# Decode attention with a cached K and V: K chunks scored in pairs, and the last output columns as one 128-wide block

## The chip, the cores and the metric

The kernel runs on one core of one Trainium2 chip. The metric is the device time in microseconds. Of the kernel before, eight runs are known: 1124.01, 1124.99, 1126.15, 1117.40, 1121.30, 1120.12, 1115.57 and 1117.45 us, with a median of 1120.71 us.

## The reference

Eight sequences (B = 8) decode one token each. The model width is D = 448, with 16 query heads, 8 key/value heads, a head size of 256, and 4096 cached positions. Two kinds of block alternate, A, B, A, B, and both A blocks use the same weights and the same caches, as do both B blocks.

```python
def A(x):                                  # x: (8, 1, 448), already normalized
    q = (x @ wq).reshape(8, 1, 16, 256)    # two query heads per key/value head
    scores = q . k_cache / sqrt(256)       # over 4096 positions
    return (softmax(scores) @ v_cache).reshape(8, 1, 4096) @ wo

def B(x):
    h  = gelu(layernorm(x) @ w1)           # then four shifts along a sequence of length 1
    x1 = x + shifted(h) @ w2               # all four shifted groups are zero: x1 = x
    return x1 + gelu(layernorm(x1) @ w3) @ w4

x = x + A(layernorm(x)); x = x + B(layernorm(x))
x = x + A(layernorm(x)); x = x + B(layernorm(x))
```

With one position per sequence each shift moves the only element out, so w1 and w2 take no part. The K and V caches have 128 MB each (134 million bytes), and both passes of A need them.

## The kernel before, in words

**Tasks and items.** There are two passes, one for each A block. A task (ps, b, gp) is pass ps, batch b and a group gp of two key/value heads; there are four groups. Each task has four K chunks and four V chunks of 128 partitions by 4096 bf16 elements, which is 1 MB. The list `items` (L534 to L543) is the order of all the work: a task's K chunks stand alternately with the V chunks of the task before. The tasks of the two passes are interleaved (L507 to L523), so that batch b's second pass comes soon after its first.

**Places.** A chunk lies in one of 15 places (`slots`, L72, `NC` = 15). Eleven chunks of each batch are `kept` (L63): all eight of group 3, and K chunks 0 to 2 of group 2. They stay in their places from the first pass to the second and are not loaded again. One more V chunk (`inner`, L64) is put into PSUM by `away` and brought back by `back`. `emit_loads` (L559) gives the next load in the list the place that has been free for the longest, and issues one DMA on SP's queue. A DMA in this queue waits for its place, and everything behind it in the queue waits too.

**A K item.** VectorE transposes the chunk in 32 by 32 blocks in two halves (`transpose_k`, L584). TensorE multiplies it with q in 32 matmuls of 8 weight columns and N = 128 (`scores`, L594), in four column groups that write to partitions 0, 32, 64 and 96. After every second chunk ScalarE takes the exponential of 256 columns (`exps`, L603). The transposition of these probabilities on TensorE (`transpose_p`, L630) and their copy to `ptw` on ScalarE (L637) are put between the halves of the next task's first scores, where `TURN` says so (L714).

**A V item.** 16 matmuls with N = 256 (`pv`, L649). The last batch's last tasks use another form (`pv_cols`, L663).

**The chain of a batch.** When two of a batch's groups are done in the first pass, `first_half` starts: the division by the sums, the transposition of the result (L412 to L447), and the product with half of wo (`add_cols`, L339). When all four are done, `chain` adds the other half, the whole B block (`mlp`) and the projection of the next q (`project_q`, L285), with a `norm` ahead of B and of the projection. A norm is a sum over partitions on TensorE (L223), small steps on VectorE, a power on GpSimd (L243) and the normalized vector `xb` (L260). These are generators: `step` (L701) advances them a step at a time between items. Each has a number of steps (11 for `first_half`, 40 for `chain`, 25 for `rest`, in the calls of `add_gen`) and a range of items over which they are spread evenly. `rest` (L495) does the product with wo and the B block for batches 0 to 3 after the second pass, once, while batch 7 is in its first pass.

**The last columns.** `add_cols` makes the 448 outputs in columns of 128 partitions: three blocks of 128 weight columns, and 64 + 64 columns for outputs 384 to 447, where the rows of PSUM are split into two halves. It yields after `every` blocks.

```python
for fc in range(5):
    lo, hi = (128 * fc, 128 * fc + 128) if fc < 3 else (384, 448)
    r = y_ps[:, fc, :] if fc < 3 else y_ps[64 * (fc - 3) : 64 * (fc - 2), 3, :]
```

The fourth column of `xT` therefore holds outputs 384 to 447 twice, and the norm's weights `wv` (L136) count each half with one half.

Of the kernel before, what the change touches and what calls it, by code (L numbers as in the profile page):

```python
# [17 lines left out]
def kernel(  # L18
# [50 lines left out]
    psum = ctx.enter_context(tc.tile_pool(name="psum", bufs=1, space=bass.MemoryType.PSUM))  # L69
    ctx.enter_context(tc.manual_schedule())  # L70

    slots = [consts.tile([128, 16 * Dh], BF16, name=f"slot{n}") for n in range(NC)]  # L72


    spare = [slots[-1], slots[-2]]
# [57 lines left out]

    wv = consts.tile([128, 4], FP32, name="wv")
    nc.vector.memset(wv[:, 0:3], 1.0 / D)
    nc.vector.memset(wv[:, 3:4], 0.5 / D)  # L136
    one = consts.tile([128, 1], FP32, name="one")
    nc.vector.memset(one[:], 1.0)
    ones = one[:].to_broadcast([128, 128])
# [44 lines left out]
    def rows_to_cols(row, nb):  # L184

        idn = identb[:nb, :nb]
        ps = room_ps("y", nb)[:, 0 : 4 * nb].rearrange("p (f b) -> p f b", b=nb)
        for fc in range(3):
            nc.tensor.matmul(
                ps[:, fc, :], row[:nb, 128 * fc : 128 * fc + 128], idn, start=True, stop=True  # L190
            )
        for r in range(2):
            nc.tensor.matmul(
                ps[64 * r : 64 * r + 64, 3, :], row[:nb, 384:448], idn, start=True, stop=True
            )
        return ps

    def norm(x, nb, twice):

        def room(name, shape, at):
            n = shape[0] * shape[1]
            if nb < Bn:
                t = chn.tile([128, n * MID], FP32, tag=name)
                ap = t[:, 0 : n * nb]
            else:
                ap = scratch(at, n * nb)
            return ap.rearrange("p (s f b) -> p s f b", s=shape[0], f=shape[1])

        def bc(ap):
            return ap.unsqueeze(1).to_broadcast([128, 4, nb])

        xx = room("xx", (2, 4), 0)
        nc.vector.tensor_mul(xx[:, 0], x, wv[:].unsqueeze(2).to_broadcast([128, 4, nb]))
        nc.vector.tensor_mul(xx[:, 1], xx[:, 0], x)
        xs = room("xs", (1, 2), 512)[:, 0]
        nc.vector.tensor_reduce(
            xs, xx.rearrange("p s f b -> p s b f"), mybir.AxisListType.X, ALU.add
        )  # L220
        yield
        st = room_ps("st", nb).rearrange("p (s b) -> p s b", b=nb)
        nc.tensor.matmul(st, ones, xs, start=True, stop=True)  # L223
        yield
        mv = room("mv", (1, 2), 528)[:, 0]
        nc.vector.tensor_copy(mv, st)
        var = room("var", (1, 1), 608)[:, 0, 0]
        if nb == 1:
            nc.vector.scalar_tensor_tensor(
                var, mv[:, 0], mv[:, 0], mv[:, 1], ALU.mult, ALU.subtract, reverse1=True  # L230
            )
        else:
            nc.vector.tensor_mul(var, mv[:, 0], mv[:, 0])
            nc.vector.tensor_sub(var, mv[:, 1], var)


        ve = room("ve", (1, 2), 544)[:, 0]
        n = 2 if twice else 1
        nc.vector.tensor_scalar(ve[:, 0], var, 0.0, EPS, ALU.max, ALU.add)
        if twice:  # L240
            nc.vector.tensor_scalar(ve[:, 1], var, 0.0, EPS * EPS / (1 + EPS), ALU.max, ALU.add)
        rs = room("rs", (1, 2), 560)[:, 0]
        nc.gpsimd.tensor_tensor(  # L243
            rs[:, 0:n].rearrange("p n b -> p (n b)"),
            ve[:, 0:n].rearrange("p n b -> p (n b)"),
            nhalf[:].to_broadcast([128, n * nb]),
            ALU.pow,
        )
        xc = room("xc", (1, 4), 576)[:, 0]
        nc.vector.tensor_tensor(xc, x, bc(mv[:, 0]), ALU.subtract)  # L250
        yield
        if nb > 1:
            yield
        c = (1 + EPS) ** -0.5 if twice else 1.0
        rl = rs[:, n - 1]
        parts = ((slice(0, 128), 0, 3, 0), (slice(0, 64), 3, 4, 3), (slice(64, 128), 3, 4, 4))
        for pp, f0, f1, to in parts:
            dst = xbs(nb)[pp, to : to + f1 - f0, :]
            if nb == 1:
                nc.vector.tensor_scalar(dst, xc[pp, f0:f1], rl[pp], c, ALU.mult, ALU.mult)  # L260
            else:
                nc.vector.scalar_tensor_tensor(
                    dst,
                    xc[pp, f0:f1],
                    c,
                    rl[pp].unsqueeze(1).to_broadcast([pp.stop - pp.start, f1 - f0, nb]),
                    ALU.mult,
                    ALU.mult,
                )
        if twice and nb == 1:  # L270
            nc.vector.scalar_tensor_tensor(x, xc, rs[:, 0], x, ALU.mult, ALU.add)
        elif twice:
            nc.vector.tensor_tensor(xc, xc, bc(rs[:, 0]), ALU.mult)
            nc.vector.tensor_add(x, x, xc)
        yield
# [51 lines left out]

    def add_cols(y_ps, rhs, w, rows, every, open=None):

        for fc in range(5):  # L330
            lo, hi = (128 * fc, 128 * fc + 128) if fc < 3 else (384, 448)
            r = y_ps[:, fc, :] if fc < 3 else y_ps[64 * (fc - 3) : 64 * (fc - 2), 3, :]
            for i in rows:
                if open is None:
                    start, stop = i == rows[0], i == rows[-1]
                else:
                    start = open[0] and fc == 0 and i == rows[0]
                    stop = open[1] and i == rows[-1]
                nc.tensor.matmul(  # L339
                    r,  # L340
                    w[:, i, lo:hi],
                    rhs(i),
                    start=start,
                    stop=stop,
                    skip_group_check=open is not None,
                )
            if fc % every == every - 1 or fc == 4:
                yield

    def mlp_hidden(b0, nb):  # L350
# [205 lines left out]
    places = list(range(NC))  # L556
    where = {}

    def emit_loads(most=None):  # L559
        n = 0  # L560
        while loads and places and n != most:
            it = loads.pop(0)
            p = where[it] = places.pop(0)
            if stays(it):
                where[tasks[it[0]][1:], it[1:]] = p
            t, kv, c = it
# [16 lines left out]
            w = t[:].bitcast(U32).rearrange("p (y e w) -> p y e w", e=2, w=64)[:, :, half]  # L583
            nc.vector.transpose(w, w)  # L584

    def scores(t, x, qbd, gp, between=None):
        kv = t[:].rearrange("p (k t e i r) -> p k e r t i", k=4, t=4, e=4, r=2)
        for n in range(8):
            half, e2, par = n // 4, (n // 2) % 2, n % 2
            if n == 4 and between is not None:  # L590
                between()
            ep = 4 * e2 + 2 * par + half
            for k in range(4):
                nc.tensor.matmul(  # L594
                    sc[32 * k : 32 * k + 8, 128 * x : 128 * x + 128],
                    qbd[:, ep, gp].rearrange("p a h -> p (a h)"),
                    kv[:, k, 2 * half + e2, par],
                    start=(n == 0),
                    stop=(n == 7),
                )  # L600
# [111 lines left out]
                    gens.remove(e)  # L712

    def TURN(n):  # L714
        return 0

    first_of = {}
    for idx, (n, kv, c) in enumerate(items):
# [3 lines left out]
    for idx, it in enumerate(items):  # L722
        n, kv, c = it
        ps, b, gp = tasks[n]
        if (ps, b, gp, kv, c) == (0, Bn - 1, REST, 0, 0):
            assert pairs_done[1, MID - 1] == 4
            add_gen("rest", 0, rest(), idx + 1, idx + 18, 25)
        p = where[(b, gp), (kv, c)] if ps == 1 and (stays(it) or inside(it)) else where[it]
        slot = slots[p]
        final = (ps, b) == (1, Bn - 1)  # L730
        if kv == 0:
# [20 lines left out]
            turn = None  # L752
            if c == TURN(n) and n - 1 in p_of:
                turn = lambda t=p_of.pop(n - 1): transpose_p(t)
            scores(slot, c, st["q"], gp, between=turn)
            if c == 1:
                p_n = work.tile([128, 4, 32, 4], BF16, tag="p_sb", bufs=1)
                p_of[n] = p_n
# [5 lines left out]
        else:  # L764
# [6 lines left out]
            if final and gp in free:  # L771
                pv_cols(oc, slot, c, gp)
                if c % 2 == 1:
# [7 lines left out]
                            lambda i: OT2[:, i % 2, i // 2, MID:],  # L781
                            wo_sb,
                            range(h0, h0 + 4),
                            5,
                            open=(claim(st), gp == free[-1] and u == 1),
                        )
                    )
# [11 lines left out]
            if c == 3:  # L799
                done = pairs_done[ps, b] = pairs_done.get((ps, b), 0) + 1  # L800
                if done == 2 and ps == 0:
                    add_gen("chain", b, first_half(b, st), idx + 1, idx + 21, 11)
                elif done == 2:
                    add_gen("chain" if final else "last", b, first_last(b, st), idx + 1, idx + 13, 9)
                elif done == 4 and ps == 0:
                    add_gen("chain", b, chain(b, st), idx + 1, first_of[(1, b), 0] - 1, 40)
                elif done == 4 and not final:
                    add_gen("last", b, last(b, st), idx + 1, idx + (7 if b == Bn - 2 else 13), 6)
        if not (ps == 0 and stays(it)):
# [18 lines left out]
    run(mlp_hidden(MID, Bn - MID))  # L828
    for q in range(4):
        for fc in range(4):  # L830
            w = 128 if fc < 3 else 64
            lo, hi = max(W * q, 128 * fc), min(W * q + W, 128 * fc + w)
            if lo < hi:
                nc.tensor.matmul(
                    o_row[32 * q : 32 * q + Bn, lo - W * q : hi - W * q],
                    xT[:w, fc, :],
                    ident2[:w, lo - 128 * fc : hi - 128 * fc],
                    start=(lo == W * q),
                    stop=False,
                    skip_group_check=True,  # L840
# [47 lines left out]
```

## Time and profile before

| | |
|---|---|
| median of eight runs | 1120.71 us |
| the profiled execution | 1124.01 us, its span 1122.2 us |
| busy: PE matmuls, PE weight loads, DVE, ACT | 716.0, 519.0, 591.7, 124.3 us |
| instructions | 36,998, of which PE 2 x 17,173 |
| read from HBM | 446.77 MB, 398 GB/s over the span |
| transposes of K chunks (L584), 400 | 469.2 us, 1219 ns each |
| matmuls of scores (L594), 8192 | 284.4 us busy |
| matmuls of V (L649), 3968 | 249.6 us busy |
| loads of K (200) and V (216), 1 MB each | 11.3 and 10.2 us from issue to landing |

How to read the profile: its page is one execution. "Busy" of an engine is the time in which at least one of its instructions runs, and PE's matmuls and weight loads (PEld) overlap. In the rows by slice each digit is a fortieth of the span in tenths. In a list in order of time a row has its start, its length, the engine, the line of the code, the operation with the names it writes and reads, the count, and in brackets the idle time before it with what ended it. "issue" there means that the engine waited for nothing that the profile shows.

### The profile page before, as it was taken

The numbers are of one execution on the slowest core, as the hardware profiler recorded it, in microseconds if no ns is written. First come the engines' busy times: TensorE is split into PE (matmuls) and PEld (weight loads), VectorE is DVE, ScalarE is ACT, GpSimd is POOL, SyncE is SP. The second block draws the span as 40 slices with busy tenths as digits, with TensorE's granted clock in tenths as the row PEclk, the third lists the DMA queues.
The fourth block names the chain that finished last, engine by engine and source line by source line (L and its number), as shares of the span: only waits on it lengthen the run. The fifth ranks groups of instructions, "written<-read, shape, count | busy, mean of one in ns | idle before, by whom it ended". The sixth has DMA issues, their size and how long they took to land. (4 is left out here: it accounts for less than half of the span.)

```text
span 1122.2 us, 36998 instructions
## 1 busy us (share of the span) xinstructions
PE 716.0 (64%) x17173; PEld 519.0 (46%) x17173; DVE 591.7 (53%) x1009; ACT 124.3 (11%) x362; POOL 15.6 (1%) x25
## 2 busy tenths in 40 slices
PE   3145577756864676636784477745778477877775
PEld 2123355434642454425563255533556355655565
DVE  5155454646465546555365553655537553485462
ACT  0001001110110011101011010110011001011010
POOL 0000000000000000000000000000000000000000
PEclk9999999655575556655556555655555555565575
DMA  9999999999999999999999999999999999999994
GB/s 357 385 419 421 410 381 404 420 411 395 419 420 420 397 410 417 420 420 385 398 419 419 420 379 403 419 420 406 402 400 419 410 396 415 418 359 398 413 418 166
DMA packets 65193, 449.15 MB, mean 400 GB/s; under 512 B 6920, under 2 KB 10896, under 8 KB 11408
## 3 DMA queue, kind: packets, MB, share of 16 engines
q1 hardware_dynamic: 65008, 446.80, 97.9%
q8 instruction: 134, 2.20, 0.8%
q14 instruction: 19, 0.16, 0.0%
q10 hardware_dynamic: 32, 0.00, 0.0%
HBM read 446.77 MB, written 0.01 MB: 398 GB/s over the span
## 5 line engine op out<-in xcount | busy, mean ns | idle before, releaser
L584 DVE STREAM_TRANSPOSE slot<-slot 128x1024 uint32<-128x1024 uint32 x400 | 469.2, 1219 | 256.1 <-DMA slot<-in_A_k_cache_dram 251.2
L594 PE MATMUL sc<-slot,qbd 128*8 128x128 bf16 x8192 | 284.4, 291 | 313.1 <-DVE slot L584 247.5
L594 PEld LDWEIGHTS <-qbd 128*8 128x8 bf16 x8192 | 191.3, 107 | 383.9 <-issue 208.3
L649 PE MATMUL o<-slot,ptw 128*8 128x256 bf16 x3968 | 249.6, 396 | 45.3 <-DMA slot<-in_A_v_cache_dram 36.2
L603 ACT ACTIVATE p_n<-sc 128x256 bf16<-128x256 f32 x128 | 95.4, 746 | 811.1 <-PE sc L594 811.1
L649 PEld LDWEIGHTS <-ptw 128*8 128x8 bf16 x3968 | 112.8, 111 | 87.1 <-issue 52.8
L339 PEld LDWEIGHTS <-wo_sb 128*128 128x128 bf16 (+1 forms) x1600 | 65.3, 123 | 25.9 <-issue 25.1
L339 PE MATMUL misc<-OT,wo_sb 128*128 128x1 bf16 (+1 forms) x1280 | 58.0, 176 | 2.7 <-issue 2.7
L285 PEld LDWEIGHTS <-wq_sb 128*128 128x128 bf16 x1152 | 34.7, 104 | 24.1 <-issue 18.6
L285 PE MATMUL misc<-xb,wq_sb 128*128 128x1 bf16 x1024 | 33.3, 166 | 3.4 <-ACT ptw L637 2.8
L311 DVE TENSOR_SCALAR qbd<-misc,quad 128x64 bf16<-128x64 f32 x64 | 13.8, 277 | 40.3 <-PE misc L305 40.3
L637 ACT CAST ptw<-misc 128x128 bf16<-128x128 f32 x64 | 17.5, 274 | 148.0 <-PE misc L630 81.7
L603 ACT ACTIVATION_READ_ACCUMULATOR p_n<-sc 128x1 f32 x128 | 33.7, 263 | 0.0
L443 PEld LDWEIGHTS misc<-R,o_sb 128*128 128x128 f32 x124 | 28.4, 316 | 10.1 <-issue 8.0
L443 PE MATMUL misc<-R,o_sb 128*128 128x8 f32 x124 | 31.3, 363 | 0.0
L339 PEld LDWEIGHTS <-w_sb 128*128 128x128 bf16 (+1 forms) x630 | 25.0, 125 | 11.0 <-issue 11.0
L243 POOL TENSOR_TENSOR t<-t,nhalf 128x2 f32<-128x2 f32 (+2 forms) x18 | 13.3, 739 | 1093.0 <-DVE t L250 1093.0
L357 PEld LDWEIGHTS <-w_sb 128*128 128x128 bf16 x560 | 18.3, 105 | 18.1 <-issue 18.1
L415 DVE RECIPROCAL rz<-misc 128x8 f32<-128x8 f32 (+1 forms) x33 | 6.3, 190 | 38.0 <-PE misc L412 36.5
L357 PE MATMUL misc<-xb,w_sb 128*128 128x1 bf16 (+1 forms) x560 | 19.2, 166 | 11.1 <-DVE xb L260 7.8
L339 PE MATMUL misc<-HT_t,w_sb 128*128 128x1 bf16 (+1 forms) x560 | 23.6, 177 | 1.6 <-DVE HT_t L380 1.5
L621 DVE STREAM_TRANSPOSE slot<-store 128x512 uint32<-128x512 uint32 x32 | 20.1, 684 | 6.4 <-PE sc L594 6.4
(94 smaller groups left out, 251.6 us busy)
## 6 DMA issues: line engine op xcount, KB each, us to landing
slot<-in_A_v_cache_dram SPq DMA_DIRECT2D x216, 1024.0 KB, 10.2
slot<-in_A_k_cache_dram SPq DMA_DIRECT2D x200, 1024.0 KB, 11.3
wo_sb<-in_A_wo_dram SPq DMA_DIRECT2D x1, 3584.0 KB, 25.7
wq_sb<-in_A_wq_dram SPq DMA_DIRECT2D x3, 1024.0 KB, 6.8
w_sb<-in_B_w_dram SPq DMA_DIRECT2D x1, 1568.0 KB, 15.6
w_sb<-in_B_w_dram SPq DMA_DIRECT2D x3, 448.0 KB, 25.6
wq_sb<-in_A_wq_dram SPq DMA_DIRECT2D x2, 256.0 KB, 9.9
w_sb<-in_B_w_dram SPq DMA_DIRECT2D x2, 112.0 KB
```

The source lines that it names most:

```text
L243: nc.gpsimd.tensor_tensor(rs[:, 0:n].rearrange("p n b -> p (n b)"), ve[:, 0:n].rearrange("p n b -> p (n b)"), nhalf[:].to_broadcast([128, ...
L285: nc.tensor.matmul(q_ps[:, j * Hq + h, :], w, xbs(nb)[:, xi, :], start=(fc == 0), stop=(fc == 3),)
L311: nc.vector.tensor_scalar_mul(qbd[:, :, :, a, :], qs.rearrange("p e (f g u h) -> p (e f) u g h", f=2, u=2, h=2)[:, :, u], quad[:, a : a + 1],)
L339: nc.tensor.matmul(r, w[:, i, lo:hi], rhs(i), start=start, stop=stop, skip_group_check=open is not None,)
L357: nc.tensor.matmul(h_ps[:, c * nb : c * nb + nb], w, xbs(nb)[:, xi, :], start=(fc == 0), stop=(fc == 3),)
L443: nc.tensor.matmul(ot_ps[:, j], o_sb[:].rearrange("p (i j) -> p j i", j=2)[:, j], R[:], start=True, stop=True)
L584: nc.vector.transpose(w, w)
L594: nc.tensor.matmul(sc[32 * k : 32 * k + 8, 128 * x : 128 * x + 128], qbd[:, ep, gp].rearrange("p a h -> p (a h)"), kv[:, k, 2 * half + e2, ...
L603: nc.scalar.activation(p_sb[:, :, :, 2 * u : 2 * u + 2].rearrange("p t i x -> p x t i"), sc[:, 256 * u : 256 * u + 256].rearrange("p (x t ...
L621: nc.vector.transpose(slot[:].bitcast(U32)[:, 512 * n : 512 * n + 512], store[n][:].bitcast(U32))
L637: nc.scalar.copy(ptw[:, :, :, 6:8], pt_ps.rearrange("p t k (a h) -> p a (t k) h", a=4),)
L649: nc.tensor.matmul(o_ps[32 * q : 32 * q + 8, 0:256], ptz[:, at : at + 8], v[:, y * Dh : (y + 1) * Dh], start=(begin and y < 4), stop=(y >= ...
```

## The change

Two edits go together.

Outputs 320 to 447 of wo and w4 become one block of 128 weight columns. `add_cols` has four blocks instead of five, the last of which starts at column 320. The fourth column of `xT` now holds outputs 320 to 447; its lower half repeats what the third column has, so its weight in the norm is 0 and the upper half's is 1/D. The norm takes the last 64 values from partitions 64 to 127.

Kept K chunks are scored in pairs. All places are slices of one tile, and where two kept chunks that are scored together lie in neighbouring places, one matmul reads both (N = 256). In the first pass the tasks of groups 2 and 3 are paired, and both chunks are scored at the odd one; in the second pass the kept pairs are scored at the even one. Where they aren't neighbours, two calls with N = 128 are made at that item. `place_for` chooses the places: for the first chunk of a pair it looks for two neighbours that are free, or will be free within four items, and reserves the second one. A load whose reserved place isn't free yet is not issued, nor are those behind it. `TURN` is 1 for the paired tasks of the first pass, and the numbers of steps are 10, 38 and 23.

```diff
-    slots = [consts.tile([128, 16 * Dh], BF16, name=f"slot{n}") for n in range(NC)]
+    PB = 16 * Dh
+    places_t = consts.tile([128, NC * PB], BF16, name="places")
+    slots = [places_t[:, n * PB : (n + 1) * PB] for n in range(NC)]
...
-    nc.vector.memset(wv[:, 3:4], 0.5 / D)
+    nc.vector.memset(wv[0:64, 3:4], 0.0)
+    nc.vector.memset(wv[64:128, 3:4], 1.0 / D)
...
-        parts = ((slice(0, 128), 0, 3, 0), (slice(0, 64), 3, 4, 3), (slice(64, 128), 3, 4, 4))
+        parts = ((0, 128, 0, 0, 3, 0), (0, 64, 64, 3, 4, 3), (64, 128, 64, 3, 4, 4))
...
     def add_cols(y_ps, rhs, w, rows, every, open=None):
-        for fc in range(5):
-            lo, hi = (128 * fc, 128 * fc + 128) if fc < 3 else (384, 448)
-            r = y_ps[:, fc, :] if fc < 3 else y_ps[64 * (fc - 3) : 64 * (fc - 2), 3, :]
+        for fc in range(4):
+            at = min(128 * fc, D - 128)
...
                 nc.tensor.matmul(
-                    r,
-                    w[:, i, lo:hi],
+                    y_ps[:, fc, :],
+                    w[:, i, at : at + 128],
                     rhs(i),
...
-            if fc % every == every - 1 or fc == 4:
+            if fc % every == every - 1 or fc == 3:
                 yield
...
+    held = {}
+    AHEAD = 4
+    def paired(n, c):
+        ps, _, gp = tasks[n]
+        u = c - c % 2
+        if ps == 0:
+            return gp in keep
+        return all((gp, 0, k) in kept for k in (u, u + 1))
...
+    def place_for(it):
+        n, kv, c = it
+        if it in held:
+            p = held.pop(it)
+            if p not in places:
+                held[it] = p
+                return None
+            places.remove(p)
+        else:
+            open_ = [p for p in places if p not in held.values()]
+            if not open_:
+                return None
+            p = open_[0]
+            if kv == 0 and c % 2 == 0 and paired(n, c):
+                two = [
+                    (max(free_at[q], now[0]), k, p1, q)
+                    for k, p1 in enumerate(open_)
+                    for q in (p1 + 1, p1 - 1)
+                    if 0 <= q < NC and q not in held.values() and free_at[q] <= now[0] + AHEAD
+                ]
+                if two:
+                    _, _, p, q = min(two)
+                    held[n, 0, c + 1] = q
+            places.remove(p)
+        free_at[p] = again[tasks[n][1:], kv, c] if tasks[n][0] == 0 and stays(it) else used_at[it]
+        return p
...
     def emit_loads(most=None):
         n = 0
         while loads and places and n != most:
-            it = loads.pop(0)
-            p = where[it] = places.pop(0)
+            it = loads[0]
+            p = place_for(it)
+            if p is None:
+                break
+            del loads[0]
+            where[it] = p
...
+                v = kv[:, k, 2 * half + e2, par]
+                if also is not None:
+                    v = bass.AP(v.tensor, v.offset, [v.ap[0], ((also - t) * PB, 2), *v.ap[1:]])
                 nc.tensor.matmul(
-                    sc[32 * k : 32 * k + 8, 128 * x : 128 * x + 128],
+                    sc[32 * k : 32 * k + 8, 128 * x : 128 * (x + nx)],
...
     def TURN(n):
-        return 0
+        return int(paired(n, 0) and tasks[n][0] == 0)
...
-            add_gen("rest", 0, rest(), idx + 1, idx + 18, 25)
+            add_gen("rest", 0, rest(), idx + 1, idx + 18, 23)
...
-            scores(slot, c, st["q"], gp, between=turn)
+            if not paired(n, c):
+                scores(p, c, st["q"], gp, between=turn)
+            elif c % 2 != ps:
+                x = c - c % 2
+                two = [p, where[(b, gp), (0, x + 1)] if ps else where[n, 0, x]]
+                if not ps:
+                    two.reverse()
+                if abs(two[1] - two[0]) == 1:
+                    scores(two[0], x, st["q"], gp, also=two[1], between=turn)
+                else:
+                    scores(two[0], x, st["q"], gp, between=turn)
+                    scores(two[1], x + 1, st["q"], gp)
...
-                    add_gen("chain", b, first_half(b, st), idx + 1, idx + 21, 11)
+                    add_gen("chain", b, first_half(b, st), idx + 1, idx + 21, 10)
...
-                    add_gen("chain", b, chain(b, st), idx + 1, first_of[(1, b), 0] - 1, 40)
+                    add_gen("chain", b, chain(b, st), idx + 1, first_of[(1, b), 0] - 1, 38)
```

## The prediction

> **What bounds the kernel now.** I read four views in this order: the page's DMA rows, busy time by stretch, the instructions in order of time, and the groups of instructions kept apart by shape.
>
> The page: the K and V loads keep the 16 DMA engines busy nearly all the time.
>
> ```profile
> PEclk9999999655575556655556555655555555565575
> DMA  9999999999999999999999999999999999999994
> GB/s 357 385 419 421 410 381 404 420 411 395 419 420 420 397 410 417 420 420 385 398 419 419 420 379 403 419 420 406 402 400 419 410 396 415 418 359 398 413 418 166
> ...
> q1 hardware_dynamic: 65008, 446.80, 97.9%
> q8 instruction: 134, 2.20, 0.8%
> ```
>
> A full slice moves 420 GB/s, so 446.8 MB need at least 1064 us and one load (1.05 MB) 2.5 us. The span is 1122.2: about 14 us lie behind the last load, some 7 at the start, and the remaining 37 or so are shallow dips. Only these 58 us can shrink. TensorE (64%) and VectorE (53%) matter only where they free a place late.
>
> The dips, by stretch (columns: stretch, length, busy us of PE, PEld, DVE, ACT, POOL, granted clock, DMA share, GB/s):
>
> ```profile
> 258.00:270.00 12.00, 7.57 (x186) 5.29 (x186) 8.67 (x19) 1.23 (x4) 0.70 (x1) 0.50 0.97 368
> ...
> 526.00:550.00 24.00, 17.91 (x404) 12.81 (x394) 14.26 (x37) 2.93 (x9) 1.26 (x2) 0.50 0.98 383
> ...
> 640.00:656.00 16.00, 10.70 (x238) 7.86 (x237) 8.85 (x16) 2.04 (x6) 0.00 (x0) 0.50 0.94 354
> ...
> 977.00:1008.00 31.00, 22.26 (x572) 15.99 (x571) 25.30 (x39) 4.68 (x14) 1.60 (x1) 0.61 0.95 364
> ```
>
> There are three kinds. The first (640 to 656, and its like in the other batches) is at the change of batch: the new batch's q has to be spread and multiplied before its first K chunk is transposed; nothing that the diff touches lies in it. The second (258 to 270, 526 to 550) is the loop that follows: four places rotate, and a V place comes free only when TensorE, working in order, has done K's scores, one step of the previous batch's chain (wo, MLP, q), then V. The third (977 to 1008) occurs once.
>
> Second kind, in order of time, around 261:
>
> ```profile
> 260.22 0.60 PE L594 MATMUL sc<-slot,qbd 128*8 128x128 bf16 x16 [0.53 <-DVE t L226]
> ...
> 261.88 0.59 PE L357 MATMUL misc<-xb,w_sb 128*128 128x1 bf16 x16 [1.06 <-DVE xb L260]
> ...
> 262.40 1.03 PE L649 MATMUL o<-slot,ptw 128*8 128x256 bf16 x16
> ...
> 263.47 0.33 SPq L576 DMA_DIRECT2D slot<-in_A_v_cache_dram  x1
> ```
>
> A chain step with its wait (1.06 + 0.59) stands between the scores and V; V's place goes to the next load only at 263.47.
>
> Third kind, the same view:
>
> ```profile
> 968.88 1.87 PE L339 MATMUL misc<-qT,wo_sb 128*64 128x4 bf16 x32
> ...
> 971.63 1.87 PE L339 MATMUL misc<-qT,wo_sb 128*64 128x4 bf16 x32
> ...
> 973.36 0.99 PE L339 MATMUL misc<-OT,wo_sb 128*64 128x1 bf16 x16
> ...
> 974.46 0.17 DVE L326 TENSOR_TENSOR xT<-xT,misc 128x16 f32<-128x16 f32 x1 [14.64 <-PE misc L339]
> ```
>
> VectorE stands 14.64 us at L326, with the transposes of landed K chunks behind it; places come back late and the loads thin out at 977 to 1008.
>
> **The change part by part.**
>
> *128-wide blocks.* By shape:
>
> ```profile
> L339 PE MATMUL misc<-OT,wo_sb 128*64 128x1 bf16 x512 | 31.9, 193 | 0.3 <-issue 0.3
> ...
> L339 PE MATMUL misc<-OT,wo_sb 128*128 128x1 bf16 x768 | 26.6, 165 | 2.4 <-issue 2.4
> ```
>
> A 64-column matmul costs 31.9/512 = 62 ns, a 128-column one 26.6/768 = 35 ns. The program has 892 of the former; 446 of the latter replace them: 55.6 - 15.4 = 40 us less PE. What reaches the end is only what lies ahead of a late release:
>
> (a) Third kind, before 974.46: two 1.87 us blocks become one of 32 matmuls (1.01), two of about 1.0 one of 0.55: 3.74 + 2.01 - 1.01 - 0.55 = 4.2 us, by which L326 and the transposes behind it come earlier; two w4 blocks at 994.4 (1.47) become 0.53. The dip lost (420 - 364)/420 x 31 = 4.1 us. I take 3.0 of it back; ends 1.0 (VectorE has 25.30 of 31 us to do whatever TensorE does) and 4.1 (there is no more).
>
> (b) Second kind. Two steps less per chain (40 to 38, 11 to 10) move the rest. In the changed program's order of a middle batch, what stands between scores and V over six K/V pairs is: (1) 32 wo matmuls, as before; (2) the norm's sum (0.59) for 16 narrow ones (1.01); (3) 32 w3 matmuls (1.01), their norm begun a V earlier, for the 1.06 + 0.59 above; (4) nothing for 8 w3 (0.37); (5) 28 w4, as before; (6) nothing for the norm's sum (about 0.9 with its wait). So V comes about 0.4, 0.6, 0.4, 0.9 us earlier, 2.3 us a batch. The stretches of this kind lost 1.0 (158 to 166, 366 GB/s), 1.5, 2.1, 1.1 (676 to 690, 386), 1.2 (808 to 822, 384), 0.3 (928 to 938, 406) and 1.1 (1008 to 1020, 380): 8.3 us. Each K still holds its place for two transposes of 1.2 us and its scores; I take half back, 4.0 us, ends 0 and 8.3.
>
> (c) The end: the last wo step is 20 matmuls (0.82 us), then 16: 0.3 us off the path behind the last load. The rearranged norm, its one memset more and one matmul less at the start hide under the first loads (0 to 0.1).
>
> *Pairs.* In the changed program 35 of 56 pairs lie in neighbouring places: 2240 matmuls of N = 128 become 1120 of N = 256. Near row at the granted 0.50: 64 with N = 128 back to back took 1.88 us (699.14), 16 with N = 256 take 1.03 (L649), 32 so about 2.0. A pair saves nothing there; at full clock (0.71 for 32, 0.61 for 16) about 0.2. The Trainium skill ("TensorE: Matmul & The Clock Gate", Back-to-back issue gap) has a cold matmul cost N/1.2 ns, so twice the columns twice the time, saving 0; its warm formula saves the fixed 2.5 ns a matmul. Reckoning instead each matmul as equally dear would have made it 35 x 1 us. I take 0. First-pass pairs also move both scores behind the odd chunk: V0 and V2 no longer stand behind K's transposes, V1 and V3 stand behind 2.0 instead of 1.03, and the transposition of p (0.29, then 0.28 on ScalarE) is bare in front of V0. Where six or seven loads are in flight this is covered by 15 us of queued loads; in batch 7 (977 to 1003) it is not: V2, freed at 994.53 after K2's scores (991.35 to 993.1), could go some 3 us earlier, V1 and V3 1 us later. Net 0, ends +2 and -2.
>
> *Fewer instructions.* 1567 matmuls with their weight loads, 3134 of 36,998 instructions, 8.5%. Their fetch is q8: 0.8% of 1122 = 9 us of DMA time, so 0.76 us. The Trainium skill ("Runtime: NRT & Kernel Launch", Instruction fetch mechanics) calls the fetch mostly hidden, which makes it 0; but here the fetch uses the resource that bounds. I take 0.7.
>
> *Places.* The reservation adds no instruction, but a load whose reserved place is still in use holds SP's queue, and all later loads, until TensorE frees it. Walking the place list through the 512 items: 15 loads get a place freed one or two items later, the load behind each then getting the earlier one. By issue and landing times, ten of them had six or seven loads in flight (one issue per landing, 2.5 us), five had two to five. 0, at most 2 us.
>
> Sum: -3.0 - 4.0 - 0.3 - 0.7 = -8.0 us on the profiled execution (1124.0, span 1122.2, 1.8 around it), which is 3.3 above the median of 1120.7. The difference carries over: 1112.7.
>
> **The rivals.**
>
> *Hidden anyway* (22%): with two loads in flight DMA is full, so an earlier release buys nothing, and the K side sets the dips. For it: the stretch 656 to 678 has 413 GB/s with the same step order. Against it: one in flight at 260.87, 527.39 and 977 to 1000. Left are 0.7 + 0.3: 1119.7.
>
> *A reserved place holds the queue* (slower, 12%). The five loads that had at most five in flight are held eight items together; if each item costs a load time, 8 x 2.5 = 20 us: 1120.7 - 8 + 20 = 1132.7. It decides from the point where the hold outlasts the loads in flight (one load in flight covers 2.5 us). Against it: in these bursts items take 0.85 to 2.2 us, and with four in flight 10 us are covered.
>
> *More comes back* (6%): all of both dips, 4.1 + 8.3, and 2 of pairs: 1105.5.
>
> **How the numbers follow.** The likeliest, 60%, is 1112.7, its own range 1108 to 1117. The shown runs scatter from 1115.6 to 1126.2, so 0.5% (5.6 us) is about what can be told from no change. Faster by more than that: most of the first case, the last one: 0.61. Within: the hidden case and the weak end of the first: 0.26. Slower: the queue case and a little for sums gone wrong: 0.13. The range has to hold the hidden case with its scatter and the stronger end: 1106 to 1123; what lies outside is the slower case and half of the 6%.
>
> **What would show it.** Right: L326's longest wait falls from 14.64 to about 10; 977 to 1008's counterpart moves over 390 GB/s; the second-kind stretches rise over 395 while the first kind stays near 354 to 374; no 64-wide shape at the add's line, some 40 us less PE busy in all; 8% fewer instruction packets; granted clock still about 0.5. Wrong: DMA rate falls in the bursts of the second pass with SP waiting for TensorE (queue case); the dips stay though releases come earlier (hidden); or pairs lengthen the wait for scores in front of V1 and V3 of batch 7.

## The result, and the profile after

The changed kernel takes 1114.53 us (median; 1107.33 to 1118.44), the kernel before 1120.09 us beside it (1112.22 to 1128.33). The ratio of the two is 0.9942 with a 95% interval of 0.9925 to 0.9960: 0.6% faster, 4.5 to 8.4 us. The forecast was 1112.7.

The profiled execution after has 1110.58 us, 4.0 below its kernel's median, while the one of before (1124.01) lies 3.9 above its own. The two pages therefore differ by 13.5 us in span, twice what the change is worth. A second trace of each kernel (below) has spans of 1116.4 before and 1114.4 after. Only what shows in both traces of a kernel is used as a finding.

From the page after, the counterparts of the rows by slice and of the DMA queues, with the busy times above them:

```profile
span 1108.7 us, 33816 instructions
...
PE 663.1 (60%) x15606; PEld 459.8 (41%) x15606; DVE 592.9 (53%) x1010; ACT 124.5 (11%) x362; POOL 15.6 (1%) x25
...
PEclk9999999655565556765565555555557555665565
DMA  9999999999999999999999999999999999999994
GB/s 358 387 421 420 417 374 408 418 419 403 409 419 421 397 412 415 419 420 401 420 420 419 421 398 407 419 419 416 406 416 420 419 400 418 419 419 399 419 419 169
...
q1 hardware_dynamic: 65008, 446.80, 98.4%
q8 instruction: 122, 2.00, 0.7%
```

The kernel is still bound by the loads: a full slice moves 420 GB/s as before, and the granted clock is about 0.5 to 0.6 in most slices. PE is busy for 52.9 us less (43.7 in the wide block alone, below, where the prediction had some 40), and 122 packets of instructions are fetched instead of 134, 9% fewer.

By stretch (same columns as before), the windows set to answer to the four stretches of the prediction, which lie 4 to 12 us earlier here:

```profile
252.00:264.00 12.00, 7.98 (x198) 5.52 (x198) 8.81 (x23) 1.01 (x3) 0.70 (x1) 0.50 0.99 386
514.00:538.00 24.00, 16.86 (x410) 11.94 (x401) 14.16 (x33) 2.93 (x9) 0.70 (x1) 0.50 1.01 407
966.00:995.00 29.00, 19.12 (x456) 12.71 (x453) 22.04 (x31) 4.61 (x14) 0.00 (x0) 0.68 1.01 419
...
636.00:652.00 16.00, 10.81 (x248) 7.69 (x236) 9.33 (x20) 2.03 (x6) 0.00 (x0) 0.50 0.98 384
```

The dip in batch 7 is gone (364 before, 419 GB/s). The two stretches of the second kind rose from 368 and 383 to 386 and 407. The stretch of the first kind, on which the change should have had no effect, rose too, from 354 to 384. The second trace of before, below, shows that rises of this size come without any change.

What VectorE waited for (us in total, times, longest), and what the queue of SP, which issues the loads, waited for:

```profile
DVE xT L325 <- PE misc L337: 19.1, 8, 8.4
```

```profile
SPq L624 <- PE o L702: 161.2, 123, 5.6
SPq L624 <- DMA places<-in_A_v_cache_dram: 146.1, 81, 3.4
SPq L624 <- DMA places<-in_A_k_cache_dram: 124.9, 62, 2.8
SPq L624 <- PE sc L647: 124.2, 132, 3.8
```

The wait of the residual add (VectorE adding the product with wo to x, L326 before, L325 after) is at most 8.4 us long instead of 14.64. The two PE rows of SP's queue are the time in which the next load stood ready and its place was still in use by TensorE: by a V product (`o`) or by scores (`sc`). In the two DMA rows it was the landing of an earlier load that ended the wait. They answer to these of before, which the prediction had not looked at:

```profile
SPq L576 <- PE o L649: 205.9, 140, 7.5
SPq L576 <- PE sc L594: 149.7, 155, 5.1
SPq L576 <- DMA slot<-in_A_v_cache_dram: 115.1, 70, 3.2
SPq L576 <- DMA slot<-in_A_k_cache_dram: 98.1, 49, 2.5
```

The PE rows together fell from 355.6 to 285.4 us, and unlike the spans their sum repeats: 355.0 in the second trace of before, 277.5 in the second one of after. But most of this wait came back under another name: the DMA rows rose from 213.2 to 271.0 (207.9 and 280.3 in the second traces). All four rows come to 568.8 and 562.9 us before and to 556.4 and 557.8 after, which is 5 to 12 us less. The largest row of SP's queue, the wait for VectorE's transposes, stayed (216.9 before, 220.8 after).

### The profile page after: what moved, and what is told of

Read it like the earlier page. It is cut to its first block, busy times and chain, and to the rows that moved or that the text cites. A ratio compares the mean times of both kernels' runs of the same rounds, so it can differ in the third digit from the quotient of the medians.

```text
span 1108.7 us, 33816 instructions
## 1 busy us (share of the span) xinstructions
PE 663.1 (60%) x15606; PEld 459.8 (41%) x15606; DVE 592.9 (53%) x1010; ACT 124.5 (11%) x362; POOL 15.6 (1%) x25
## 5 line engine op out<-in xcount | busy, mean ns | idle before, releaser
L632 DVE STREAM_TRANSPOSE places<-places 128x1024 uint32<-128x1024 uint32 x400 | 469.1, 1218 | 275.7 <-DMA places<-in_A_k_cache_dram 275.6
L647 PE MATMUL sc<-places,qbd 128*8 128x128 bf16 (+1 forms) x7072 | 268.9, 305 | 293.3 <-DVE places L632 247.7
L647 PEld LDWEIGHTS <-qbd 128*8 128x8 bf16 x7072 | 168.5, 105 | 368.6 <-issue 183.8
L702 PE MATMUL o<-places,ptw 128*8 128x256 bf16 x3968 | 242.9, 388 | 103.3 <-DMA places<-in_A_v_cache_dram 85.7
L337 PEld LDWEIGHTS <-wo_sb 128*128 128x128 bf16 x1280 | 38.6, 102 | 21.6 <-issue 21.3
L337 PE MATMUL misc<-OT,wo_sb 128*128 128x1 bf16 x1024 | 34.7, 165 | 2.0 <-issue 2.0
L241 POOL TENSOR_TENSOR t<-t,nhalf 128x2 f32<-128x2 f32 (+2 forms) x18 | 13.3, 739 | 1079.1 <-DVE t L248 1079.1
L674 DVE STREAM_TRANSPOSE places<-store 128x512 uint32<-128x512 uint32 x32 | 20.1, 685 | 11.5 <-PE sc L647 11.5
L410 PE MATMUL misc<-zm,one 128*128 128x8 f32 (+1 forms) x66 | 19.1, 362 | 4.2 <-ACT ptw L690 2.4
L355 PE MATMUL misc<-xb,w_sb 128*128 128x1 bf16 (+1 forms) x560 | 18.6, 166 | 4.1 <-DVE xb L261 2.9
L410 PEld LDWEIGHTS misc<-zm,one 128*128 128x128 f32 x66 | 16.2, 304 | 10.9 <-ACT o_sb L436 3.7
L445 DVE CAST OT<-misc 128x16 bf16<-128x16 f32 x16 | 2.4, 152 | 33.5 <-PE misc L441 30.8
```

The lines of the kernel that those rows point to most:

```text
L337: nc.tensor.matmul(y_ps[:, fc, :], w[:, i, at : at + 128], rhs(i), start=start, stop=stop, skip_group_check=open is not None,)
L355: nc.tensor.matmul(h_ps[:, c * nb : c * nb + nb], w, xbs(nb)[:, xi, :], start=(fc == 0), stop=(fc == 3),)
L410: nc.tensor.matmul(z_ps, ones, zm[:], start=True, stop=True)
L647: nc.tensor.matmul(sc[32 * k : 32 * k + 8, 128 * x : 128 * (x + nx)], qbd[:, ep, gp].rearrange("p a h -> p (a h)"), v, start=(n == 0), sto ...
L674: nc.vector.transpose(slot[:].bitcast(U32)[:, 512 * n : 512 * n + 512], store[n][:].bitcast(U32))
L702: nc.tensor.matmul(o_ps[32 * q : 32 * q + 8, 0:256], ptz[:, at : at + 8], v[:, y * Dh : (y + 1) * Dh], start=(begin and y < 4), stop=(y >= ...
```

## The experiments

All ratios are to the kernel before, run beside each kernel on the same chip, with a 95% interval; the medians of before there were 1120.77 us for the wide and narrow blocks and for pairs alone, 1119.85 for the order and for the pairs of the second pass, and 1119.79 for the places and the last three rows. Two numbers were worked out from the traces, with the loads counted from 0. A landing is the end of a load's last packet. The *excess in batch 7* is the time from the landing of load 368 to that of load 376 less eight times 2.49 us, the interval of landings at full rate. The *excess, second kind* is the same for the loads that span the prediction's seven stretches of this kind in the first trace of before: 48 to 52, 87 to 92, 191 to 201, 249 to 255, 300 to 306, 346 to 351 and 376 to 382.

| kernel | ratio | median us | VectorE's longest wait at the residual add | excess in batch 7 | excess, second kind | SP waiting for TensorE (`o` and `sc`) |
|---|---|---|---|---|---|---|
| before, two traces | 1 | 1120.09 | 14.6 | 4.3, 4.2 | 9.5, 3.0 | 355.6, 355.0 |
| after, two traces | 0.9942 [0.9925, 0.9960] | 1114.53 | 8.4 | 0.3, 0.3 | 5.8, 5.7 | 285.4, 277.5 |
| wide block alone | 0.9968 [0.9942, 0.9993] | 1117.48 | 9.8 | 1.2 | 3.8 | 300.6 |
| pairs alone | 0.9967 [0.9946, 0.9988] | 1116.52 | 11.6 | 1.8 | 10.7 | 311.0 |
| wide block, old steps | 0.9967 [0.9944, 0.9990] | 1116.41 | 11.1 | 0.8 | 5.1 | 325.3 |
| narrow blocks, new steps | 0.9979 [0.9947, 1.0011] | 1120.94 | 13.3 | 4.3 | 4.2 | 322.2 |
| order of pairs alone | 0.9995 [0.9970, 1.0019] | 1118.38 | 12.9 | 3.3 | 4.3 | 328.3 |
| pairs of the second pass alone | 0.9944 [0.9920, 0.9968] | 1115.45 | 12.1 | 3.2 | 5.3 | 313.2 |
| places alone | 1.0014 [0.9990, 1.0037] | 1121.45 | 14.6 | 4.0 | 7.3 | 355.5 |
| after, q early | 0.9966 [0.9937, 0.9996] | 1115.21 | 9.2 | 0.2 | 4.0 | 284.7 |
| wide block, pairs of the second pass | 0.9957 [0.9929, 0.9985] | 1113.55 | 7.8 | 0.3 | 4.9 | 281.3 |
| the same, q early | 0.9939 [0.9916, 0.9963] | 1112.11 | 7.8 | 0.3 | 5.1 | 281.6 |

**Second traces.** The kernels before and after once more, without an edit, since the two pages differ by more than the change can.

> The kernel before once more, for a second trace of it. The profiled execution of before took 1124.0 us, 3.3 above its median, and three variants with quite different edits all land their loads some 4 us ahead of that trace by load 368, so the trace itself is suspected. If it is: this one lies near the median (1118 to 1121), with about 4 us less lost in the loops, and batch 7's stretch (load 368 to 376) as long as before (24.3 us). If not: the loops' gain is real.

> The changed kernel once more, for a second trace: its first profiled execution took 1110.6 us, 4 below its median. Batch 7's stretch (load 368 to 376) should again be about 20.3 us; if the loops' gain was luck, the landings are again 5 to 8 us ahead of an ordinary trace of before and not 13.

The one of before took 1118.13 us, the one of after 1116.16. The second trace of before, by stretch, for the first kind and for batch 7:

```profile
636.00:652.00 16.00, 9.38 (x210) 6.77 (x211) 8.56 (x16) 2.05 (x6) 0.00 (x0) 0.50 0.99 394
971.00:1002.00 31.00, 22.53 (x580) 15.99 (x572) 26.11 (x43) 4.69 (x14) 1.64 (x1) 0.61 0.95 367
```

And the second trace of after, for batch 7:

```profile
966.00:995.00 29.00, 19.85 (x486) 13.34 (x477) 24.17 (x43) 4.11 (x12) 1.64 (x1) 0.67 1.01 419
```

Batch 7 is the same as in the first traces: 364 and 367 before, 419 twice after. The first kind isn't: its stretch reads 354 GB/s in the first trace of before and 394 in the second, for the same program. So a dip of the first kind is deeper or shallower from one execution to the next, and its rise to 384 after is no finding. The same holds for the second kind. Over the loads of its seven stretches the second trace of before lost 3.0 us where the first lost 9.5, and the two of after, 5.8 and 5.7, lie between (526 to 550: 0.1 instead of 2.3). The stretches had been picked as the dips of one trace, and a second trace has its dips elsewhere. What the change does to the second kind can therefore not be read from these traces; only batch 7 can.

**One part alone.** The first question was which of the two edits brings the gain. The wide block alone is the kernel before with this and its norm, and the new numbers of steps:

```diff
-        for fc in range(5):
-            lo, hi = (128 * fc, 128 * fc + 128) if fc < 3 else (384, 448)
+        for fc in range(4):
+            at = min(128 * fc, D - 128)
...
-            if fc % every == every - 1 or fc == 4:
+            if fc % every == every - 1 or fc == 3:
                 yield
...
-            add_gen("rest", 0, rest(), idx + 1, idx + 18, 25)
+            add_gen("rest", 0, rest(), idx + 1, idx + 18, 23)
...
-                    add_gen("chain", b, first_half(b, st), idx + 1, idx + 21, 11)
+                    add_gen("chain", b, first_half(b, st), idx + 1, idx + 21, 10)
...
-                    add_gen("chain", b, chain(b, st), idx + 1, first_of[(1, b), 0] - 1, 40)
+                    add_gen("chain", b, chain(b, st), idx + 1, first_of[(1, b), 0] - 1, 38)
```

> The kernel before with the 128-wide block for the last columns (four blocks, steps 10, 38, 23) and nothing of the pairs. Theory (the blocks bring it, the pairs only fetch less): within 1 us of the changed kernel, about 1115 us, ratio to before 0.995. Rival (the pairs bring it): about 1119 us, ratio 0.999.

Pairs alone is the kernel before with the rest of the change: the one tile for all places, `place_for` and its reservations, the scores of two chunks and `TURN`; blocks and steps stay as they were.

> The kernel before with the pairs and the reserved places and nothing of the blocks (five blocks, steps 11, 40, 25). Theory: 2240 instructions less to fetch and nothing else, about 1119.5 us, ratio 0.9995. Rival (the pairs bring it): about 1115 us, ratio 0.995. If a reserved place holds the queue: 1122 us or more.

Each brings 0.3%, and the sum of both, 0.65%, agrees with the 0.58% of the change. Both theories missed: the wide block, reckoned at nearly all of the gain (0.995), measured 0.9968, and pairs, reckoned at nothing (0.9995), measured 0.9967. In batch 7 the wide block alone moves VectorE's wait from 14.6 to 9.8 us and takes 3.1 us of the dip (4.3 and 4.2 to 1.2). Pairs alone take 2.4 of the same dip (to 1.8), so there the two can't add: 4.0 is all that goes with both. The wait in the wide block alone:

```profile
DVE xT L323 <- PE misc L335: 20.5, 8, 9.8
```

**Is it the shorter block or the moved steps?** The prediction named both for the second kind. The wide block with the old steps gets an empty fifth step, so that each later step of a chain stands where it stood:

```diff
             if fc % every == every - 1 or fc == 3:
                 yield
+        if every < 4:
+            yield
```

> The 128-wide block, no pairs, but with one empty step behind it, so that a chain has its old 11, 40 and 25 steps and they fall where they fell before. Theory: the stretch of batch 7 (3.0 us) and the end (0.3) come back, of the loops' 4.0 us only what the narrower blocks themselves cost there (about 1): 1116 us, ratio 0.996. If the order of steps doesn't matter: as with the blocks alone.

The narrow blocks with the new steps keep all matmuls of the kernel before (two groups of 64 columns), but do the two in one step, and take the numbers 10, 38 and 23:

```diff
-        for fc in range(5):
-            lo, hi = (128 * fc, 128 * fc + 128) if fc < 3 else (384, 448)
+        for fc in range(4):
+            blocks = [(128 * fc, 0, 128)] if fc < 3 else [(320, 0, 64), (384, 64, 128)]
+            for at, p0, p1 in blocks:
```

> The two 64-wide blocks kept, made in one step, so that the steps number 10, 38 and 23 and fall where the changed kernel has them; no pairs. Theory: of the loops' 4.0 us about 3 come back, nothing in batch 7's stretch: 1117 us, ratio 0.997. If the number of steps doesn't matter: as before, 1120 us.

The wide block with the old steps is as fast as with the new (0.9967 and 0.9968). It takes 3.5 us of the dip in batch 7. With the narrow blocks the dip in batch 7 is there as before. In order of time, the two narrow blocks of that kernel in batch 7:

```profile
964.20 3.39 PE L336 MATMUL misc<-qT,wo_sb 128*64 128x4 bf16 x64
967.52 1.02 PE L646 MATMUL o<-slot,ptw 128*8 128x256 bf16 x16
968.47 1.68 PE L336 MATMUL misc<-OT,wo_sb 128*64 128x1 bf16 x32
```

TensorE's narrow blocks are all there, now in two lumps (5.07 us; 5.75 in before), and the residual add waits 13.3 us. So in batch 7 it is the shorter block that counts, not the steps moved. In the second kind this stays open, since its excess (5.1 and 4.2 us in these two kernels) scatters by more between two traces of one kernel. By time alone nothing is settled either: the narrow kernel's interval (0.9947 to 1.0011) holds both nothing and the whole effect of the wide block.

**Which part of pairs?** Three kernels take it apart. All have the five blocks and old steps of before, and their cuts show what differs from pairs alone. Order alone scores the kept chunks where the changed kernel does, but in two calls, and reserves no place:

```diff
-            if kv == 0 and c % 2 == 0 and paired(n, c):
+            if False:
...
-                if abs(two[1] - two[0]) == 1:
+                if False:
```

> Pairs without merging and without reservations: the places are given as before and every pair is two calls with N = 128, but at the items at which the pairs stand. It tells the order from the merging. If the pairs' gain is their order in the first pass (V0 and V2 ahead of K's scores in batch 7): ratio about 0.997, as with the pairs whole, and load 368 to 376 in about 22 us. If it is the merging (fewer instructions, less PE): about 1.000.

Places alone has the one tile for all places and the reservation, and scores each chunk at its own item, with `TURN` at 0, as before:

```diff
-            if not paired(n, c):
+            if True:
```

> The kernel before with the changed choice of places and its reservations, but no pair is merged or moved: every chunk is scored alone, at its own item. If the choice of places brings the pairs' gain: ratio 0.996. If merging brings it (fewer instructions, fewer long stops of TensorE at issue): 1.000, with some 26 stops over 0.8 us as before. If a reservation holds the queue: above 1.000.

The pairs of the second pass alone merges there, and leaves the first pass and `TURN` as they were:

```diff
-            elif c % 2 != ps:
+            elif ps == 0:
+                scores(p, c, st["q"], gp, between=turn)
+            elif c % 2 == 0:
```

> Pairs in the second pass alone: the places are reserved as in the changed kernel, the second pass's neighbours are scored in one matmul, and the first pass scores each chunk at its own item as before; no blocks. If the pairs' gain is the order in the first pass: 0.9995, load 368 to 376 in about 24 us. If it is the merging: 0.998 or less.

The places alone do nothing (1.0014; a loss above 0.4% is excluded), and the order alone does nothing that can be told (0.9995), though it takes 0.9 us off the dip in batch 7. The second pass alone, with 16 merged pairs, is no worse than all 35 (0.9944 against 0.9967; the intervals overlap), and its interval lies outside those of order alone and of places alone. So it is merging that brings the gain of pairs, as far as these intervals can tell. In groups kept apart by shape, the scores of this kernel:

```profile
L651 PE MATMUL sc<-places,qbd 128*8 128x128 bf16 x7168 | 248.2, 288 | 308.3 <-DVE places L636 266.4 <-issue 18.6 <-ACT p_n L660 6.6
L651 PE MATMUL sc<-places,qbd 128*8 128x256 bf16 x512 | 30.7, 409 | 10.7 <-DVE qbd L313 6.1 <-ACT p_n L660 4.6
```

A merged pair keeps TensorE busy for 30.7/16 = 1.92 us, two single calls for 2 x 248.2/224 = 2.22: 0.30 us a pair, 4.8 in all. The idle time before scores that is put down to "issue" is 18.6 us here and 27.1 in the same group of before, but it is 18.3 with order alone too. It has large single members. In order of time, in the dense scoring of the second pass of before:

```profile
711.96 0.48 PE L594 MATMUL sc<-slot,qbd 128*8 128x128 bf16 x10 [2.23 <-issue]
...
719.39 0.59 PE L594 MATMUL sc<-slot,qbd 128*8 128x128 bf16 x15 [1.87 <-issue]
```

TensorE stops for about 2 us in the middle of 32 matmuls that, by these rows, wait for nothing. Such stops of over 0.8 us number 27 (42.0 us) and 26 (41.4) in the two traces of before, 25 (37.3) for order alone and 27 (47.6) for places alone; pairs alone has 13 (26.2), the second pass alone 16 (30.4), after 15 (28.1) and 13 (21.5).

The single packets in the traces tell what they wait for. Each of the 27 stops of the first trace of before ends 1.27 to 1.60 us after a packet of the queue q8, the instruction fetch, has landed: the one before 719.39 us ends 1.49 us after such a landing. In all 14 traces this holds for 281 stops of 281, with 1.20 to 1.63 us, while of matmuls picked at regular intervals only 7 or 8 in 100 start 1.2 to 1.7 us behind one. So what TensorE waits for there is its instructions. Two of them stand in VectorE's long wait of batch 7, here in the first trace of before:

```profile
961.38 0.48 PE L594 MATMUL sc<-slot,qbd 128*8 128x128 bf16 x9 [1.63 <-issue]
...
967.59 0.40 PE L339 MATMUL misc<-qT,wo_sb 128*128 128x4 bf16 x9 [1.24 <-issue]
```

Of the 14.6 us of that wait 2.9 and 2.2 us are such stops in the two traces of before. In pairs alone it is 1.0 of 11.6, so about half of the 3.0 us that pairs take off the wait are shorter stops. In the two traces of after 4.1 and 4.0 of 8.4 us are stops. Their number alone doesn't set the time: the narrow blocks with new steps have 17 (30.9 us), and are not clearly faster, and the last kernel of the table has 25 (40.0) and the lowest median.

**The first kind.** These dips (10.6 and 9.3 us of excess over six stretches in the two traces of before, loads 236 to 242 and their like) were put down to q, which is spread late. The changed kernel with q of a new batch's first task spread four items ahead:

```diff
+        for n2, kv2, _ in items[idx + 1 : idx + 5]:
+            ps2, b2, _ = tasks[n2]
+            if kv2 == 0 and ps2 == 0 and (0, b2) not in state:
+                q2 = work.tile([128, 8, GP, 4, 2], BF16, tag="qbd", bufs=3)
+                run(spread_q(qT1[:, :, b2], q2))
+                state[0, b2] = {"q": q2}
```

> The changed kernel with the spreading of a new batch's first-pass q (16 matmuls and 4 steps of VectorE) put four items earlier, ahead of the first kind of dip. If that dip is the late spreading, as the prediction has it: half of the 9 us lost there come back, 1110 us, ratio to before 0.991. If four rotating places set it anyway: as the changed kernel, 0.994 to 0.995.

Nothing came of it: 0.9966, where 0.991 had been hoped for, with the excess of the first kind 7.3 us beside 6.6 and 8.1 in the two traces of after. The explanation falls for this kernel; the dips of the first kind are left without one.

**Combined.** Since the second pass alone gave as much as all pairs, as far as can be told, the changed kernel with the first pass scored at its own items, and then that with q early too:

> The changed kernel, but with the first pass's chunks each scored at its own item; the second pass's pairs and the blocks stay. If the first pass's pairs give something (V0 and V2 earlier in batch 7): slower than the changed kernel by 1 us or more, ratio 0.996. If they give nothing or cost something: 0.993 or less, and batch 7's stretch (load 368 to 376) still in about 21 us.

> The run before and the early spreading of q together. If both are worth what they are hoped to be: 0.988 to 0.990, faster than either kernel; if neither is: 0.994 to 0.996.

They came to 0.9957 and 0.9939. Both intervals overlap with that of the change (0.9925 to 0.9960), so neither is shown to be better or worse, and what the first pass's pairs are worth stays open. The dip in batch 7 is gone in both (0.3 us), and SP waits as long for TensorE as in the two traces of after.

## Why the prediction was right, point by point

**The sign and the size.** Forecast were -8.0 us and 1112.7; measured were -5.6 by medians and about -6.5 by the ratio. The likeliest case came, at the weaker side of its own range. Of its two large terms the first is shown, the second isn't, and pairs, put at nothing, brought alone as much as the wide block alone. That a term too large and one too small met is luck.

**(a) The third kind: right.** The term was 3.0 of a dip of 4.1. The wide block alone takes 3.1. Both traces of after show 4.0 taken (4.3 and 4.2 to 0.3), near the upper end; the last 0.9 are the pairs'. The wait fell by 6.2 us, not 4.2, and the runs say why: the wide block takes 4.8 off it (14.6 to 9.8) and pairs 3.0 (14.6 to 11.6); with both it falls to 8.4. The lower end, VectorE having 25.30 of 31 us of its own to do, didn't bind.

**(b) The second kind: not shown.** The forecast was 4.0 of 8.3 us. Over the same loads the two traces of before lose 9.5 and 3.0, those of after 5.8 and 5.7, so an effect of 4.0 could not be seen, and none is. The step that failed is to take the dips of a single trace for dips of the kernel. The kernels that were to tell the shorter blocks from the moved steps can't do so here either, so that "two steps less per chain move the rest" and the four earlier releases of V are neither shown nor refuted. The bar of 395 GB/s set for these stretches was passed in one (407) and missed in one (386; 401 in the second trace).

**The two in time.** The wide block alone was worth -3.0 - 4.0 - 0.3 = -7.3 us by the sum, and took 0.32% or 3.6 us (0.8 to 6.5). That is about its 3.1 us in batch 7; the interval leaves room for some of the second kind, but not for the whole sum. The whole change took 4.5 to 8.4 us, a little more than the 4.0 of batch 7; where the rest of it lies is not known.

**(c) The end: not seen.** 14.6 us lie behind the last load before and after; the 0.3 is 0.1 at most.

**Pairs: the term that was mis-sized.** "I take 0" was said of merging, since 16 matmuls with N = 256 take 1.03 us at the granted 0.50 and 64 with N = 128 took 1.88. Pairs alone measured -0.33%, 3.7 us (1.3 to 6.0), where the sum had 0, and +2 to -2 for their order. The nearest row was the wrong one: a run of 64 in a row has one start and one end, while the single calls stand apart. In place, two calls of 32 cost 2.22 us and a merged pair 1.92, as shown above. From order alone to pairs alone the busy time of the scores fell by 7.0 us (277.6 to 202.8 + 67.8), 0.2 a pair, and PE's whole by 12.8 (715.6 to 702.8). The Trainium skill's rule that a cold matmul costs N/1.2 ns ("TensorE: Matmul & The Clock Gate", Back-to-back issue gap) made 0 of it as well, but the section gives it for a single matmul by itself; the runs here give 0.2 to 0.3 us for each pair. For the changed kernel that is 7 to 10 us of TensorE time, spread over the whole span. Where it reaches the end can be seen in one place: pairs alone lose 1.8 us in batch 7 instead of 4.3 and 4.2, of which order alone gives 0.9. The prediction had looked at that place and had the pairs' gains and losses cancel there. It isn't the whole account: the second pass alone takes only 1.1 us there, and 6.3 us (3.6 to 9.0) in time.

**The order of pairs: right, at 0.** Order alone is 0.9995 [0.9970, 1.0019]. In batch 7, where V2 was to go earlier, 0.9 us less was lost; at the end nothing is seen of it.

**Fewer instructions: reckoned at the wrong engine.** Packets fell from 134 to 122 (9% fewer; 8% had been said) and their share of DMA from 0.8% to 0.7%, so the 0.7 us of DMA time may be right, and no run here can resolve it. But the fetch also stops TensorE, for 42.0 and 41.4 us in the two traces of before and 28.1 and 21.5 in those of after, and the prediction had no term for that. The Trainium skill calls the fetch "mostly hidden" ("Runtime: NRT & Kernel Launch", Instruction fetch mechanics). By number that agrees: 27 of the 134 packets of before have a stop of over 0.8 us behind them. How much of these stops reaches the end isn't known beyond batch 7.

**Places, and the rival of the reserved place: refuted.** Places alone is 1.0014 with at most +0.4%, 4.1 us, where the rival asked for 20. The longest wait of SP's queue for a V product is 7.7 us there, 7.5 before. In the changed kernel it is 5.6.

**Hidden anyway: refuted.** It had DMA full with two loads in flight, so that the K side sets the dips, and left 1.0 us of gain; at least 4.5 came. The dip of batch 7 went when the releases came earlier. What each kernel's trace loses less in batch 7 than before lies inside the interval of its time for eight of the eleven kernels of the table: 3.1 us for the wide block, 2.4 for pairs, 3.5 for the wide block with old steps, 0 for the narrow blocks, 0.9 for the order, 0.2 for the places. The whole change and the last row gain a little more in time (4.0 us in batch 7 for both, at least 4.5 and 4.1 in time), the pairs of the second pass much more. SP's waiting for TensorE goes along nearly as well, with 0.07 to 0.08 us of time for each of its microseconds (70 to 78 for 5.6 in the change), and it too gives less than was measured for the pairs of the second pass (3.2 us instead of 3.6 to 9.0). Both are regularities of these kernels, not mechanisms shown.

**What would have shown it wrong.** The first kind was to stay at 354 to 374 GB/s; it reads 384 in the trace of after. Taken as a sign, it would have spoken against the account; the second trace of before (394) shows that the sign itself was no good.

## What to carry to other kernels

Take a second trace of the same program before a dip in one profile is given a cause or a worth: two of the three kinds of dip here changed as much with nothing changed as with the edit, and the one that repeated to 0.1 us, batch 7's, is the one that can be argued from. In a kernel that the loads bind, read what the load queue waits for and by whom, and sum it: that number repeats within 3% where spans differ by 6 us. Read all its rows, though, since a wait that is taken from one engine can come back under another name. The price of a matmul is to be read where its calls stand, with their starts and ends, since a long run of them shows the inside only.

## What was not expected of the hardware

TensorE stops in the middle of a run of matmuls, mostly for 1 to 3 us: 27 and 26 times in the two traces of before, 41 to 42 us together, in eight bursts, one for each batch. By the rows it waits for nothing, but each stop ends 1.2 to 1.6 us after a packet of instructions has landed. One packet came for every 256 matmuls and weight loads (median, before). One of the longest, from the order of time of pairs alone:

```profile
715.84 1.01 PE L651 MATMUL sc<-places,qbd 128*8 128x128 bf16 x29 [2.97 <-issue]
```

A kernel at full load rate spreads over 1.0 to 1.4% between executions of the same program (1112 to 1128 us before). Batch 7's dip was alike to 0.1 us in two traces; the loads from 24 on without it lost 34.9 and 29.4 us, which is nearly all of the 5.8 us between the two spans.
